# GFNet mixer and gated MLP on one core: one raw-weight subtraction moves behind three unfolding differences in GpSimd's order

## The chip, the cores and the metric

The kernel runs on one core of a Trainium2 chip. The metric is the device time of one execution in microseconds (us). The time before is the median of three executions, 441.07 us, the lowest 440.99 and the highest 441.2.

Engines are named as the profile names them: PE is TensorE's matrix multiplication and PEld its weight load, DVE is VectorE, ACT is ScalarE, POOL is GpSimd and SP is SyncE, which issues the DMAs.

## The reference

The input is 2048 rows of 512 numbers. The first half of the layer normalises the rows, filters them in the frequency domain and adds the input; the second half normalises again and adds a gated MLP.

```python
x = A_x
h = x + irfft2(rfft2(layernorm(x)) * (w_r + 1j * w_i), s=(S, D))     # S, D = 2048, 512
g, u = layernorm(h) @ w_gate, layernorm(h) @ w_up                    # 512 -> 1376
h2 = h + (gelu(g) * u) @ w_down                                      # 1376 -> 512
```

## The kernel before, in words

The 2048 rows are 16 blocks of 128 rows. The Fourier transforms are matrix products with tables of cosines and sines, and symmetries of the tables halve them: sums and differences of the two halves of a row ("folding") are transformed, and the two parts of the result are put together again by sums and differences ("unfolding"). The MLP's hidden width of 1376 is cut into 11 tiles of 128. Products of two-by-two tiles are done with seven products in place of eight, so each tile of gate and up weights needs four sums and differences of the raw weights first (`load_gu`, lines 194 to 229), and then every operand is split into a high and a low part.

The order of the instructions on PE, ACT, DVE and POOL is written out by hand, in strings of short names. `START` orders the forward transform over the rows, `SECOND` the filter and the transform back over the rows, and `FIRST` the transform back over the columns, the second normalisation and the first products of the MLP. A name issues one step; what the steps put on one engine runs in the order of the list. Which instruction waits for which is worked out by the framework from the buffers. SP has its own order, which the framework's scheduler sets.

The change lies in the first line of `FIRST`, where the inverse transform over the columns begins. For a block `b` of rows (0 to 7), in the order in which one needs the other:

- `u`/`w` (two halves) or `U` (whole): the transform of block `b` on PE (L530), 8 instructions in the profile for a whole block, into PSUM bank `k` of `U1.2` (block 1, bank 2).
- `C`: ACT copies the bank into a row buffer (L856).
- `V`: DVE forms one half of the unfolded row from the bank and that copy (L864).
- `X`: POOL forms the other half, a difference, from the copy (L887).
- `M`: PE multiplies the unfolded row by the table `mis` (L869), 2 instructions in the profile, into bank `k` of `M4.1`. It needs both halves, and the bank must have been read by `C` and `V` of the block that had it.
- `O`: ACT copies the odd half of the product (L874); `H`: DVE adds the residual (L879); `G` and `I`: POOL unfolds once more into `gh` (L883).

The names `r0`, `r1`, `r2`, `r3` and `lo1` to `lo3` prepare the third tile of gate and up weights, step by step:

```python
    raw2 = load_gu(2, by=act)
    next(raw2)
    for k in ("r0", "r1", "r2", "r3", "lo1", "lo2", "lo3"):
        do[k] = lambda: next(raw2)
```

The first `next` issues the two DMAs of the tile on SP, 256 KB each (L200, L201), into the single buffer `raw`, which the second tile has used until then: its last read is a split on POOL (L157). Then `r0` is one POOL instruction, the difference of the first column of the raw tile (L207):

```python
        with held("late"):
            pooled["raw"] = i = pool.tensor_tensor(t[:, 4], t[:, 0], t[:, 3], op=ALU.subtract)
```

The next of these names, `r1`, stands far down in the list. `pooled["raw"]` is read again by `late(b)`, which loads a row block for the last stage: its DMA (L975) is made to come behind the newest raw difference.

Of the kernel before, what the change touches and what calls it, by code (L numbers as in the profile page):

```python
# [46 lines left out]
ROOTS = {0: 1, 1: 1, 2: 2, 4: 4, 8: 4, 12: 4}  # L47

FIRST = """
u4.0 w4 u0.1 r0 C4.0 w0 C0.1 U1.2 C1.4 U5.3 C5.5 V4.2 X4 V0.3 X0 M4.1 O4.0 V1.0 M0.2 O0.1 X1 V5.1 X5 H4 G4 H0 I4 U2.3  # L50
C2.5 V2.3 M5.1 U7.2 H5 C7.1 S4 O5.0 G0 A4 g0awh I0 S0 A0 M1.3 O1.1 Q0 U3.4 E0.5 V7.4 X2 C3.5 U6.0 C6.0 N0 R01 I5 R00
H1 G5 S5 X7 M2.1 V6.3 H2 G1 I1 S1 X6 U8.4 C8 T01.2 s0.0 O2.1 l0 T00 A5 A1 c0 V3.1 Q1 M7.0 O7.0 E1.6 U9.7 a0 N1 R10
M6.4 T10 X3 I2 d0 e0.1 k0 H7 H6 f0 g0 b0 h0 U12.3 G2 R11 T11.1 a1 I7 M3.2 C12 U15.3 b1 g0aP0 s1.2 c1 i0 G7 O3.1 O6.0
# [1377 lines left out]
```

## Time and profile before

| | |
|---|---|
| median of three executions | 441.07 us |
| the profiled execution's own time | 440.65 us |
| its span, first to last instruction | 438.4 us |
| PE busy | 432.1 us (99%) |
| POOL busy | 314.3 us (72%) |
| DVE busy | 311.2 us (71%) |
| ACT busy | 244.2 us (56%) |
| granted TensorE clock, mean | 1.000 |

All times of single instructions below come from that one profiled execution and count from its first instruction. A row of a timeline has the start, the duration, the engine, the line of the kernel, the operation, what it writes and reads, and how many instructions of that kind are merged into the row; the bracket at the end is the time for which the engine stood idle before it, and what ended that. An engine named with a q behind it is its queue of waits. A row of the chain of waits has the start, the duration, the engine, the tile and the line.

### The profile page before, as it was taken

The page shows a single profiled execution, that of the slowest core. Times are in us where ns is not written, and L with a number is a line of the kernel's source. Part 1 is how long each engine was busy: PE and PEld are TensorE (multiplying, and loading weights), DVE is VectorE, ACT ScalarE, POOL GpSimd, SP SyncE. Part 2 cuts the span into 40 slices and gives each one's busy share as a digit, 9 for nine tenths or more (in the row PEclk, how much of TensorE's full clock was granted, in tenths as well). Part 3 has the DMA queues.
Part 4 walks back from the last instruction along what each step waited for, and adds up shares of the span by engine and source line. Part 5 has one row for each costly group of instructions (what it writes and reads, how often), then busy time and mean ns, then how long its engine had stood idle before and what let it go on. Part 6 is the DMA issues. An engine that isn't in the chain of part 4 may idle for free.

```text
span 438.4 us, 6627 instructions
## 1 busy us (share of the span) xinstructions
PE 432.1 (99%) x2275; PEld 366.3 (84%) x2275; DVE 311.2 (71%) x576; ACT 244.2 (56%) x505; POOL 314.3 (72%) x346
## 2 busy tenths in 40 slices
PE   8999999999999999999999999999999999999996
PEld 8998999789978777877888888888888888888885
DVE  5968976798764766368734579578677787687786
ACT  5989785699912442124432687376455653565640
POOL 6987896999958788648652944067879779787821
PEclk9999999999999999999999999999999999999999
DMA  8996904320032112112220203501212121200005
GB/s 290 387 414 98 364 22 151 126 73 25 1 120 97 49 49 96 48 49 72 72 73 24 73 25 120 169 9 64 73 48 73 28 70 49 72 25 2 0 2 192
DMA packets 23542, 41.60 MB, mean 95 GB/s; under 512 B 4178, under 2 KB 9810, under 8 KB 23380
## 3 DMA queue, kind: packets, MB, share of 16 engines
q1 hardware_dynamic: 23220, 40.92, 27.8%
q8 instruction: 18, 0.29, 0.3%
q10 hardware_dynamic: 288, 0.26, 0.2%
q14 instruction: 16, 0.13, 0.1%
HBM read 36.97 MB, written 4.20 MB: 94 GB/s over the span
## 4 chain that ended last, share of the span: by engine, by line
PE 92%; ACT 3%; DVE 2%; DMA 1%; issue 1%; POOL 0%; DVEq 0%; POOLq 0%
PE ps L165 16%; PE ps L163 16%; PE ps L164 16%; PE ps L769 14%; PE ps L1108 11%; PE ps L425 4%; PE ps L437 3%; PE ps L530 3%; PE ps L464 3%; PE ps L869 2%; PE ps L977 1%; ACT ts L380 1%; PE ps L1214 1%; DMA gh<-in_x 1%; PE ps L563 1%; PE ps L569 1%
## 5 line engine op out<-in xcount | busy, mean ns | idle before, releaser
L163 PE MATMUL ps<-cb,gu 128*128 128x512 f32 (+1 forms) x336 | 127.4, 379 | 0.0
L165 PE MATMUL ps<-cb,gu 128*128 128x512 f32 (+1 forms) x336 | 124.9, 372 | 0.0
L164 PE MATMUL ps<-cb,gu 128*128 128x512 f32 (+1 forms) x336 | 124.8, 371 | 0.0
L673 ACT ACTIVATE s<-ps 128x512 f32<-128x512 f32 (+1 forms) x72 | 40.2, 560 | 87.5 <-PE ps L165 87.2
L228 POOL TENSOR_TENSOR gu<-raw,gu 128x768 fp32r<-128x768 f32 (+1 forms) x42 | 61.3, 1480 | 29.6 <-DVE gu L223 17.0
L164 PEld LDWEIGHTS ps<-cb,gu 128*128 128x128 f32 x336 | 63.3, 188 | 11.7 <-issue 1.0
L163 PEld LDWEIGHTS ps<-cb,gu 128*128 128x128 f32 x336 | 63.3, 188 | 11.7 <-issue 1.0
L165 PEld LDWEIGHTS ps<-cb,gu 128*128 128x128 f32 x336 | 63.3, 188 | 11.0
L769 PE MATMUL ps<-wd,a 128*128 128x512 f32 x264 | 63.5, 392 | 0.0
L769 PEld LDWEIGHTS ps<-wd,a 128*128 128x128 f32 x264 | 49.2, 188 | 11.5 <-DVE gh L978 0.9
L682 DVE TENSOR_TENSOR ps<-ps,s 128x512 f32<-128x512 f32 (+1 forms) x48 | 31.2, 651 | 27.4 <-PE ps L165 25.3
L1115 DVE TENSOR_TENSOR gh<-ps,gh 128x512 f32<-128x512 f32 x66 | 44.1, 680 | 1.0 <-PE ps L1108 1.0
L679 ACT ACTIVATE s<-s 128x512 f32<-128x512 f32 (+1 forms) x48 | 28.5, 594 | 20.9 <-DVE s L676 20.9
L775 DVE TENSOR_TENSOR gh<-ps,gh 128x512 f32<-128x512 f32 x24 | 16.5, 689 | 27.0 <-PE ps L769 26.9
L676 DVE TENSOR_TENSOR s<-ps,s 128x512 f32<-128x512 f32 (+1 forms) x48 | 30.7, 640 | 5.8 <-PE ps L165 4.7
L511 POOL TENSOR_TENSOR wd<-wdr,wd 128x512 fp32r<-128x512 f32 x12 | 15.5, 1295 | 19.1 <-ACT wd L509 19.1
L676 DVE TENSOR_TENSOR ps<-ps,s 128x512 f32<-128x512 f32 (+1 forms) x24 | 15.7, 653 | 16.8 <-ACT s L673 16.6
L207 POOL TENSOR_TENSOR raw<-raw 128x256 f32<-128x256 f32 x16 | 11.8, 738 | 16.7 <-DMA raw<-in_wgu 15.0
L1021 POOL TENSOR_TENSOR t<-mis,t 128x768 fp32r<-128x768 f32 (+1 forms) x9 | 13.3, 1480 | 13.2 <-ACT t L1019 13.2
L688 ACT ACTIVATE a<-ps 128x512 fp32r<-128x512 f32 (+1 forms) x26 | 13.7, 532 | 15.6 <-DVE ps L682 15.6
L429 ACT ACTIVATE dp<-ps 64x512 f32<-64x512 f32 x32 | 18.9, 591 | 4.1 <-PE ps L425 3.7
L453 POOL TENSOR_TENSOR z<-t,t 128x520 f32<-128x520 f32 x15 | 19.4, 1295 | 2.1 <-DVE t L445 2.1
(183 smaller groups left out, 896.4 us busy)
## 6 DMA issues: line engine op xcount, KB each, us to landing
wt<-in_w SPq DMA_DIRECT2D x16, 520.0 KB, 7.7
raw<-in_wgu SPq DMA_DIRECT2D x32, 256.0 KB, 3.0
out<-gh SPq DMA_DIRECT2D x15, 256.0 KB, 2.0
gh<-in_x SPq DMA_DIRECT2D x7, 512.0 KB, 8.8
row<-in_x SPq DMA_DIRECT2D x12, 256.0 KB, 2.8
wdr<-in_wd SPq DMA_DIRECT2D x12, 256.0 KB, 2.7
mis<-in_wd SPq DMA_DIRECT2D x10, 256.0 KB, 2.6
a<-in_wgu SPq DMA_DIRECT2D x8, 256.0 KB, 3.1
```

What stands on the lines that cost most here:

```text
L163: pe.matmul(o, lh, rh, start=(i == 0 and not onto), stop=False, skip_group_check=True)
L164: pe.matmul(o, lh, rl, start=False, stop=False, skip_group_check=True)
L165: last = pe.matmul(o, ll, rh, start=False, stop=(i == n - 1), skip_group_check=True)
L228: pooled["lo"] = pool.tensor_tensor(r[:, 1, m], t[:, m], r[:, 0, m].bitcast(F32), op=ALU.subtract)
L453: eng.tensor_tensor(z[:, :, first], t1[:, :, first], t2[:, :, first], op=ALU.add)
L673: return lambda: act.activation(to, a, AF.Copy)
L676: return lambda: dve.tensor_tensor(to, a, b, op=ALU.add)
L679: return lambda: act.activation(g, g, AF.Gelu_apprx_tanh)
L682: return lambda: dve.tensor_tensor(u, u, g, op=ALU.mult)
L769: pe.matmul(o, parts_of[tiles.index((0, f))][:, ha, i // 4, r], wds[f][:, hw, c], start=start, stop=stop)
L1108: pe.matmul(ps[:, k], w[:, hw], a[ha], start=start and hw + ha == 0, stop=hw == 1, skip_group_check=True)
L1115: by.tensor_tensor(to, o, to, op=ALU.add)
```

## The change

`r0` moves within the first line of `FIRST`, from a place ahead of `X4`, `X0` and `X1` to a place behind them and ahead of `X5`.

```diff
 FIRST = """
-u4.0 w4 u0.1 r0 C4.0 w0 C0.1 U1.2 C1.4 U5.3 C5.5 V4.2 X4 V0.3 X0 M4.1 O4.0 V1.0 M0.2 O0.1 X1 V5.1 X5 H4 G4 H0 I4 U2.3
+u4.0 w4 u0.1 C4.0 w0 C0.1 U1.2 C1.4 U5.3 C5.5 V4.2 X4 V0.3 X0 M4.1 O4.0 V1.0 M0.2 O0.1 X1 r0 V5.1 X5 H4 G4 H0 I4 U2.3
```

On POOL, at the start of the inverse transform over the columns, this is the order before. `gu_97` is the second weight tile's split, `raw_922` the third tile's raw weights, `row_…` are the row buffers of `X4`, `X0`, `X1` and `X5` in this order, and the `gh` rows are `G4`, `I4`, `G0` and `I0`; the brackets have the engines and DMA queues that a row waits for.

```order
L157 TENSOR_TENSOR gu_97<-raw_584,gu_97 128x256 [waits Activation_49]
L207 TENSOR_TENSOR raw_922<-raw_922 128x256 [waits DMAHW4_49,DMAHW3_49,Pool_49]
L887 TENSOR_TENSOR row_899<-row_897 128x2x128 [waits Activation_49]
L887 TENSOR_TENSOR row_900<-row_898 128x2x128 [waits Activation_49]
L887 TENSOR_TENSOR row_897<-row_901 128x2x128 [waits DVE_49,Activation_49,Pool_49]
L887 TENSOR_TENSOR row_898<-row_902 128x2x128 [waits DVE_49,Activation_49,Pool_49]
L883 TENSOR_TENSOR gh_58<-a_894,t_921 128x256 [waits DMAHW6_49,DVE_49]
```

The same place on POOL in the changed kernel:

```order
L157 TENSOR_TENSOR gu_97<-raw_584,gu_97 128x256 [waits Activation_49]
L887 TENSOR_TENSOR row_899<-row_897 128x2x128 [waits Activation_49]
L887 TENSOR_TENSOR row_900<-row_898 128x2x128 [waits Activation_49]
L887 TENSOR_TENSOR row_897<-row_901 128x2x128 [waits DVE_49,Activation_49,Pool_49]
L207 TENSOR_TENSOR raw_922<-raw_922 128x256 [waits DMAHW4_49,DMAHW3_49]
L887 TENSOR_TENSOR row_898<-row_902 128x2x128 [waits DVE_49,Activation_49,Pool_49]
L883 TENSOR_TENSOR gh_58<-a_894,t_921 128x256 [waits DMAHW6_49,DVE_49]
```

L207 has moved behind three of the L887 rows; it still waits for the two DMAs, and the L887 rows wait for what they waited for.

On SP, the order of the DMAs is the same, and one wait is added. This is the piece of the difference there; `row_1496` is the row block of the first `late`.

```order
 L803 DMA a_894<-in_x 128x512 [waits DMAHW0_49]
 L506 DMA wdr_982<-in_wd 128x512 [waits DMAHW1_49]
-L975 DMA row_1496<-in_x 128x512 [waits DMAHW2_49,PE_49]
+L975 DMA row_1496<-in_x 128x512 [waits DMAHW2_49,PE_49,Pool_49]
 L975 DMA row_1503<-in_x 128x512 [waits DMAHW3_49,DVE_49,Pool_49]
```

The first L975 now waits for POOL as well, that is for L207 in its new place. PE, ACT and DVE have the same rows with the same waits as before.

## The prediction

> **What bounds the kernel now.** I read the page first, then the chain of waits, then the timelines of the engines around the moved instruction. The page says that TensorE is busy throughout and that the chain that ended last is almost wholly its own.
>
> ```profile
> span 438.4 us, 6627 instructions
> PE 432.1 (99%) x2275; PEld 366.3 (84%) x2275; DVE 311.2 (71%) x576; ACT 244.2 (56%) x505; POOL 314.3 (72%) x346
> ...
> PE 92%; ACT 3%; DVE 2%; DMA 1%; issue 1%; POOL 0%; DVEq 0%; POOLq 0%
> ```
>
> So a microsecond counts only where PE waits. The chain of waits between 73 and 80 us has one of its few places where it leaves PE for ACT and POOL, and it is the place of the change:
>
> ```profile
> 74.21 2.96 PE ps L530 x24
> ...
> 77.19 0.61 ACT row L856
> ...
> 77.83 0.42 POOL row L887
> ...
> 78.29 1.98 PE ps L869 x4
> ```
>
> PE's product for block 4 (M4, L869) starts when POOL's first unfolding difference (X4, L887) is done. POOL's timeline shows why that is so late:
>
> ```profile
> 72.34 0.73 POOL L157 TENSOR_TENSOR gu<-raw,gu 128x256 fp32r<-128x256 f32 x1
> 76.82 0.73 POOL L207 TENSOR_TENSOR raw<-raw 128x256 f32<-128x256 f32 x1 [3.76 <-DMA raw<-in_wgu]
> 77.51 2.78 POOL L887 TENSOR_TENSOR row<-row 128x256 f32<-128x256 f32 x4
> 80.70 1.42 POOL L883 TENSOR_TENSOR gh<-a,t 128x256 f32<-128x256 f32 x2 [0.40 <-DVE a L879]
> ```
>
> POOL stands for 3.76 us at r0 (L207), until the raw weights of the third tile have landed at 76.82. Behind it queue the four differences X4, X0, X1 and X5, one every (2.78 - 0.73) / 3 = 0.68 us. The DMA can't come earlier: it waits for the buffer that L157 reads until 73.07, and SP issues it from 73.09.
>
> ```profile
> 73.09 0.33 SPq L200 DMA_DIRECT2D raw<-in_wgu  x1
> 73.46 0.43 SPq L201 DMA_DIRECT2D raw<-in_wgu  x1
> 74.01 1.82 SPq L803 DMA_DIRECT2D a<-in_x  x4
> ...
> 79.45 9.40 SPq L975 DMA_DIRECT2D row<-in_x  x2
> ```
>
> **The change, part by part.** Nothing is added or removed: one POOL subtraction of 0.73 us moves behind X1. What the differences then wait for is ACT's copies (L856: C4, C0, C1, C5 in this order) and, for X5, DVE's half (L864: V4, V0, V1, V5):
>
> ```profile
> 75.41 0.60 ACT L856 ACTIVATE row<-ps 128x512 f32<-128x512 f32 x1 [1.25 <-PE ps L530]
> 76.30 0.60 ACT L856 ACTIVATE row<-ps 128x512 f32<-128x512 f32 x1 [0.30 <-PE ps L530]
> 77.19 0.60 ACT L856 ACTIVATE row<-ps 128x512 f32<-128x512 f32 x1 [0.30 <-PE ps L530]
> 78.08 0.60 ACT L856 ACTIVATE row<-ps 128x512 f32<-128x512 f32 x1 [0.30 <-PE ps L530]
> 79.45 0.38 ACT L874 ACTIVATE t<-ps 128x256 f32<-128x256 f32 x1 [0.77 <-PE ps L869]
> ```
> ```profile
> 76.03 0.42 DVE L864 TENSOR_TENSOR row<-ps,row 128x256 f32<-128x256 f32 x1 [1.43 <-ACT row L856]
> 76.93 0.42 DVE L864 TENSOR_TENSOR row<-ps,row 128x256 f32<-128x256 f32 x1 [0.47 <-ACT row L856]
> 78.27 0.42 DVE L864 TENSOR_TENSOR row<-ps,row 128x256 f32<-128x256 f32 x1 [0.92 <-POOL row L887]
> 78.96 0.42 DVE L864 TENSOR_TENSOR row<-ps,row 128x256 f32<-128x256 f32 x1 [0.26 <-POOL row L887]
> 79.87 1.61 DVE L879 SCALAR_TENSOR_TENSOR a<-a,mv,ps 128x512 f32<-128x512 f32 x2 [0.49 <-ACT t L874]
> ```
>
> The copies end at 76.01, 76.90, 77.79 and 78.68. A consumer starts 0.02 to 0.04 us behind (DVE 76.03 behind 76.01). So X4 runs from 76.05 to 76.78 (it ended at 78.24 before), X0 from 76.94 to 77.67, X1 from 77.83 to 78.56, and V1 and V5, which in the rows waited 0.92 and 0.26 us for POOL, start at 77.83 and 78.72 and end at 78.25 and 79.14. r0 comes next, when its data have been there since 76.82: 78.51 to 79.24, one pitch of 0.68 behind X1. X5 runs from 79.20 to 79.93, where it started at 79.57 and ended at 80.29 before. DVE beside POOL costs nothing extra: V0 at 76.93 ran beside r0 and took 0.42 like V4, which had POOL idle beside it.
>
> X4 is thus no longer what M4 waits for, and what is late next is PE itself. Where PE goes from a transform to a product without a wait, the product starts 0.22 us behind the start of the last transform instruction (80.78 to 81.00), and its two instructions take 0.43 each (81.00 to 81.86). At M4 the last transform instruction started at 77.77:
>
> ```profile
> 77.77 0.28 PE L530 MATMUL ps<-dis,gh 128*128 128x128 f32 x1
> ...
> 78.82 1.45 PE L869 MATMUL ps<-row,mis 128*128 128x512 f32 x3
> ```
> ```profile
> 80.78 0.39 PE L530 MATMUL ps<-dis,gh 128*128 128x128 f32 x2
> ...
> 81.00 1.02 PE L869 MATMUL ps<-row,mis 128*128 128x512 f32 x2
> ...
> 81.86 0.38 PE L530 MATMUL ps<-dis,gh 128*128 128x128 f32 x2
> ```
>
> So M4 starts at 77.99, its second instruction at 78.42 instead of 78.82, M0 at 78.85 and the transform of block 2 at 79.71 where this row has 80.11:
>
> ```profile
> 80.11 1.05 PE L530 MATMUL ps<-dis,gh 128*128 128x128 f32 x8
> ```
>
> **The gain on PE is 0.40 us.** Each cover holds: V0 frees M4's bank at 77.35; M0 needs X0 (77.67) and V1 (78.25), and has until 78.85; the transform of block 2 needs V5 (79.14), and has until 79.71; M5 needs X5, and its weight load stood at 80.89, now 80.49, 0.56 us behind X5's new end. If X1 also had to wait for V1, X5 would end at 80.40, still in time.
>
> The residuals (L879) follow the products: ACT's L874 stood 0.63 behind M4's second instruction, and L879 0.42 behind that, so H4 moves from 79.87 to 79.47, and POOL's L883 from 80.70 to 80.30. POOL is there in time, done with X5 at 79.93. H4 also needs its block of the input, the second of the four L803 transfers, whose landings are in this row:
>
> ```profile
> DMA to landing us min/median/max: 4.2/4.6/4.8
> ```
>
> Landings count from an issue's end (L201's: 73.89 + 2.9 = 76.79, and r0 started at 76.82). The second issue of the four ends near 74.01 + 1.82 / 2 = 74.92; with the median of 4.6 the block is there at 79.5. H4 may so lose 0.05 us, which is hidden: the next L879 on DVE waits for M0's odd half, 0.40 behind M4's.
>
> SP: the first L975 now waits for r0 too, done at 79.24, and for M4, which moves to about 79.05. It is issued at 79.3 instead of 79.45, and the second L975 comes 9 us later anyway. The data of the first are used at 124.91, so even half a microsecond more would cost nothing.
>
> Is the gain given back later? These rows are the busy time by stretches (length; PE, PEld, DVE, ACT, POOL; then granted clock, DMA share and GB/s), the waits of PE from 78 us to the end, and of PEld from 100 us on:
>
> ```profile
> 74.21:78.29 4.08, 3.84 (x32) 3.65 (x33) 1.26 (x4) 2.00 (x4) 1.47 (x3) 1.00 0.92 306
> 78.29:94.40 16.11, 16.11 (x98) 12.09 (x99) 14.41 (x36) 13.00 (x31) 15.49 (x23) 1.00 0.26 85
> ```
> ```profile
> PE ps L869 <- POOL row L887: 0.2, 1, 0.2
> ```
> ```profile
> PEld ps L769 <- DVE gh L978: 0.9, 1, 0.9
> ```
>
> POOL works 15.49 of 16.11 us in the stretch behind the change, so it might have become the bound; but it starts that stretch 0.4 us earlier like PE, and PE waits for nobody. The one later wait of 0.9 us is for DVE's L978, and the chain puts a PE product right ahead of it, so it moves along:
>
> ```profile
> 123.95 0.87 PE ps L977 x2
> ...
> 124.91 0.76 DVE gh L978
> ```
>
> Sum: span 438.4 - 0.4 = 438.0, the profiled execution 440.65 - 0.40 = 440.25. The median of the runs lies 0.42 us above the profiled execution; carried over, 441.07 - 0.40 = **440.67 us**, 0.09% less. A measurement of this kernel can tell about 0.2% (0.88 us) from no change, so this counts as within it.
>
> **What is not known** is when the raw weights land in an ordinary execution. The gain is 0.40 plus what they land later than here, and nothing if they land 0.4 us earlier. The transfers into this buffer around the change took this long, and those of L201 over the whole kernel this long:
>
> ```profile
> DMA to landing us min/median/max: 2.7/2.9/3.7
> ```
> ```profile
> DMA to landing us min/median/max: 3.0/3.1/7.7
> ```
>
> Here it was 2.9. With 2.7 the gain is 0.20, with 3.7 it is 1.20. I take 2.9, this very transfer's.
>
> A rule that speaks against the gain: the Trainium skill, "DMA: Bandwidth & Descriptors", section "Anatomy of one DMA — SWDGE (gpsimd) path", fits a transfer's time as about 2.0 us plus the bytes over 436 GB/s. For 256 KB an estimate by that page is 2.6 us, 0.3 less than the trace's 2.9, and the gain would be 0.10. The fit is for another path of issue and for a transfer alone, so the trace's own duration is used.
>
> **Rivals.**
>
> *Most of the gain isn't there* (gain 0 to 0.25, about 440.95): the transfer lands earlier in ordinary executions, as the shortest of 2.7 would, or PE catches up with POOL's nearly full queue in the stretch from 78.29 to 94.40. For it: 15.49 of 16.11 us busy. Against it: no wait of PE for POOL in that stretch behind M4 and M0. The page's 2.6 us is of this kind.
>
> *The gain is larger* (over 0.88, about 440.0): the transfer is later in ordinary executions; by the 3.7 of the longest into this buffer the kernel before loses 1.20 us and the changed one still nothing, since r0 has until 78.5. For it: the median is 0.42 above the profiled execution. Against it: that may lie anywhere in the kernel.
>
> *Slower:* r0 still waits, now with X5 and the residual's unfolding behind it. M5's weight load stood at 80.89, so X5 must end by 80.84 and r0 start by 79.42; a landing 2.6 us later than here decides. With the longest of L201, 7.7 us, 4.8 more, r0 starts at 81.62, X5 ends 1.41 later at 83.03, and M5 comes 2.2 us later than before: 443.3. For it: r0 stands at the head of POOL's queue all the same, and the DMA engines are 92% busy from 74.21 to 78.29. Against it: the order of the DMAs doesn't change, so nothing new is ahead of this transfer, and with the same lateness the kernel before would have lost more.
>
> *The move has no effect*, since X4 waits for something that r0 waited for too. The order of instructions speaks against it: X4 waits for ACT alone, whose copy was done at 76.01.
>
> **How the numbers follow.** The forecast of 0.25 to 0.88 us gained 0.67; most of the gain absent 0.17; no effect 0.01; larger 0.09; slower by over 0.2% 0.06. That makes faster 0.09, same 0.85, slower 0.06. The range leaves out the slower case and most of the larger one: from a gain of 0.9 to no gain and 0.13 for the spread of the runs before, 440.15 to 441.2.
>
> **What would show it.** In the changed profile L207 starts near 78.5 and waits for no DMA; X4 starts near 76.05 behind ACT's copy; PE has no idle time ahead of L869, and its second instruction starts near 78.42; the first L975 is issued near 79.3; the later stages keep their lengths and the span is 438.0. I am wrong if L869 still waits (then for which half?), if PEld waits for X5 near 80.5, or if a wait of about 0.4 us appears between 80 and 125 us.

## The result, and the profile after

The changed kernel takes 440.28 us (median of 22 executions, 439.98 to 440.93) against 441.03 us of the kernel before (22 executions, 440.66 to 441.46). The ratio is 0.9984 with a 95% interval of 0.9977 to 0.9991: 0.75 us between the medians, 0.4 to 1.0 us by the interval. That is faster, but by less than 0.2%. The prediction had 440.67, in a range from 440.15 to 441.2.

Times below count from S, the start of PE's first transform instruction (L530) of this stage, because S itself moves by a few tenths of a microsecond from one execution to the next whatever the kernel (74.13 to 74.45 us in the profiles here). S is 74.21 in the profile before and 74.45 in the profile after.

POOL in the profile after, from the last split of the second weight tile to the first residual unfoldings:

```profile
72.59 0.72 POOL L157 TENSOR_TENSOR gu<-raw,gu 128x256 fp32r<-128x256 f32 x1
76.32 0.73 POOL L887 TENSOR_TENSOR row<-row 128x256 f32<-128x256 f32 x1 [3.01 <-ACT row L856]
77.22 0.73 POOL L887 TENSOR_TENSOR row<-row 128x256 f32<-128x256 f32 x1 [0.17 <-ACT row L856]
78.17 0.73 POOL L887 TENSOR_TENSOR row<-row 128x256 f32<-128x256 f32 x1 [0.22 <-POOL row L887]
78.85 0.72 POOL L207 TENSOR_TENSOR raw<-raw 128x256 f32<-128x256 f32 x1
79.53 0.73 POOL L887 TENSOR_TENSOR row<-row 128x256 f32<-128x256 f32 x1
80.44 2.79 POOL L883 TENSOR_TENSOR gh<-a,t 128x256 f32<-128x256 f32 x4 [0.17 <-DVE a L879]
```

X4, X0 and X1 now follow ACT's copies, r0 has no wait in front of it, and X5 is done at S + 5.81. PE:

```profile
74.45 3.84 PE L530 MATMUL ps<-dis,gh 128*128 128x128 f32 x32
78.13 1.88 PE L869 MATMUL ps<-row,mis 128*128 128x512 f32 x4
79.85 1.05 PE L530 MATMUL ps<-dis,gh 128*128 128x128 f32 x8
80.74 1.02 PE L869 MATMUL ps<-row,mis 128*128 128x512 f32 x2
```

L869 has lost the idle time in its bracket. The **stretch** from S to the transform behind M0 is 79.85 - 74.45 = 5.40 us, where the profile before had 80.11 - 74.21 = 5.90. The chain of waits goes from the transforms to the products without leaving PE:

```profile
74.45 3.84 PE ps L530 x32
78.29 1.72 PE ps L869 x4
80.01 0.89 PE ps L530 x8
```

Up to DVE's L978, the later wait that the prediction named, nothing is given back: from the transform behind M0 to there it is 124.91 - 80.11 = 44.80 us before and 124.66 - 79.85 = 44.81 after. From the same transform to PE's last group of products (L1214) it is 433.06 - 80.11 = 352.95 us before and 432.94 - 79.85 = 353.09 after, so 0.1 us comes back in the rest of the kernel; why is not shown. First the two rows of the profile before, then those of the profile after:

```profile
124.91 0.75 DVE L978 SCALAR_TENSOR_TENSOR gh<-row,mv,ps 128x512 f32<-128x512 f32 x1 [1.54 <-PE ps L977]
433.06 1.55 PE L1214 MATMUL ps<-a,wd 128*128 128x512 f32 x9
```
```profile
124.66 0.75 DVE L978 SCALAR_TENSOR_TENSOR gh<-row,mv,ps 128x512 f32<-128x512 f32 x1 [1.54 <-PE ps L977]
432.94 1.55 PE L1214 MATMUL ps<-a,wd 128*128 128x512 f32 x9
```

So the mechanism is the one predicted. One number doesn't fit: the stretch is 0.50 us shorter in these two profiles, and the medians are 0.75 us apart.

### The profile page after: what moved, and what is told of

The parts are those of the page before. It is cut to its first block, busy times and chain, and to the rows that moved or that the text cites. A ratio compares the mean times of both kernels' runs of the same rounds, so it can differ in the third digit from the quotient of the medians.

```text
span 438.3 us, 6627 instructions
## 1 busy us (share of the span) xinstructions
PE 432.5 (99%) x2275; PEld 367.0 (84%) x2275; DVE 311.2 (71%) x576; ACT 244.3 (56%) x505; POOL 314.9 (72%) x346
## 4 chain that ended last, share of the span: by engine, by line
PE 92%; POOL 4%; DMA 1%; issue 1%; DVE 1%; ACT 0%; SPq 0%; DVEq 0%
PE ps L163 16%; PE ps L165 16%; PE ps L164 16%; PE ps L769 14%; PE ps L1108 11%; PE ps L425 4%; PE ps L530 3%; PE ps L437 3%; PE ps L464 3%; POOL pn L339 2%; POOL pn L338 2%; PE ps L869 2%; PE ps L977 1%; PE ps L1214 1%; DMA gh<-in_x 1%
## 5 line engine op out<-in xcount | busy, mean ns | idle before, releaser
L207 POOL TENSOR_TENSOR raw<-raw 128x256 f32<-128x256 f32 x16 | 11.8, 737 | 12.9 <-DMA raw<-in_wgu 11.2
```

## Experiments

The theory: M4 waited for X4, X4 for r0, and r0 for the landing of the raw weights; once X4 passes r0, PE sets the pace and nothing is given back. The rivals: r0's own 0.73 us of work was the cost, and not the wait; every difference that passes r0 gives a share, because POOL's queue is what counts; the wait only moves and comes back at X5; and, for the missing 0.25 us, something apart from this edge. Each run was timed beside the kernel before on the same chip (median 441.00 to 441.03 us).

| run | r0 or its stand-in starts, us behind S | stretch, us | median, us | ratio to the kernel before |
|---|---|---|---|---|
| kernel before, four profiles | 2.61, 2.75, 2.86, 3.14 | 5.90, 6.03, 6.15, 6.43 | 441.03 | 1.0001 (0.9992 to 1.0009), run again |
| changed kernel, two profiles | 4.40, 4.39 | 5.40, 5.39 | 440.28, 440.21 | 0.9984 (0.9977 to 0.9991), 0.998 (0.997 to 0.9989) |
| behind_x4 | 3.02 | 5.45 | 440.21 | 0.9979 (0.997 to 0.9989) |
| work_alone | -1.06 | 5.40 | 440.11 | 0.9975 (0.9964 to 0.9986) |
| wait_alone | 3.06 | 5.81 | 440.52 | 0.9984 (0.9975 to 0.9993) |
| late_old | 3.79 | 7.07 | 441.31 | 1.0005 (0.9996 to 1.0014) |
| late_new | 4.39 | 5.39 | 439.83 | 0.9974 (0.9964 to 0.9984) |
| behind_x5 | 5.29 | 5.39 | 440.10 | 0.9981 (0.9972 to 0.999) |
| behind_i0 | 8.71 | 5.39 | 440.72 | 0.9995 (0.9985 to 1.0004) |
| far_back | after this stage | 5.40 | 440.11 | 0.9979 (0.997 to 0.9988) |

The medians hold 2.2 us that lie outside the span of the instructions, but 1.8 to 1.9 us in work_alone, wait_alone and far_back and 2.1 us in the two late runs. In the profiles of the first three the span also goes on for 3.4 us behind the last output's issue (L1220) instead of 3.1, so their medians come out about 0.1 us low. The cause of this is open; where a median and the stretch differ by as little, the stretch is the safer measure.

### The changed kernel once more

No edit.

> The changed kernel once more, beside the runs below on one chip. Theory (M4 waited for X4, X4 for r0): PE comes from the first transform instruction (L530) to the transform behind M0 in 5.40 us again, where the kernel before takes 5.90, and the time is 0.5 to 0.75 us under the kernel before. Rival (the 0.75 us of the medians holds something besides this edge): the stretch is 5.40 us again, and the time still lies 0.25 us or more further down than the stretch explains.

Measured: stretch 5.39 us, 440.21 us, 0.82 us under the kernel before. The stretch is the theory's. The time lies 0.32 us further down than this stretch and the first profile's 5.90 explain, which is what the rival asked for; the profiles of the kernel before, below, show where that comes from.

### Which difference has to pass r0

```diff
-... V4.2 X4 V0.3 X0 M4.1 O4.0 V1.0 M0.2 O0.1 X1 r0 V5.1 X5
+... V4.2 X4 r0 V0.3 X0 M4.1 O4.0 V1.0 M0.2 O0.1 X1 V5.1 X5
```

> r0 stands behind X4 alone, ahead of X0, X1 and X5. Theory (only the edge from X4 to M4 counts): X0 ends near the time at which X4 ended before, 0.6 us ahead of M0's need, so the stretch is 5.40 us and the time that of the changed kernel, within 0.15 us. Rival (every difference that passes r0 gives its share, since POOL's queue is what counts): a third of the gain, 0.2 us, and two thirds are lost.

Measured: 440.21 us, the changed kernel's time, and a stretch of 5.45. POOL's rows in this run:

```profile
76.02 0.72 POOL L887 TENSOR_TENSOR row<-row 128x256 f32<-128x256 f32 x1 [3.01 <-ACT row L856]
77.16 0.73 POOL L207 TENSOR_TENSOR raw<-raw 128x256 f32<-128x256 f32 x1 [0.42 <-DMA raw<-in_wgu]
77.84 2.11 POOL L887 TENSOR_TENSOR row<-row 128x256 f32<-128x256 f32 x3
```

r0 waits for its DMA again, 0.42 us, and X0, X1 and X5 stand behind it; X0 ends at S + 4.4, only 0.1 us ahead of M0's start where 0.6 was expected, and the stretch is 0.05 us longer. The gain comes with X4. Shares per difference are out. But the landing still stands ahead of X0 in this order, and here it let r0 start at S + 3.02: a later one, such as the S + 3.14 of one profile below, would reach M0 through X0. That is an estimate from these rows; no run shows it.

### The work without the wait, and the wait without the work

Both put a stand-in `rx` into r0's old place, with r0 in its new one. The first subtracts data that are there already, and r0 overwrites its result; the second subtracts two columns of the raw tile:

```diff
-u4.0 w4 u0.1 C4.0 w0 C0.1 ...
+u4.0 w4 u0.1 rx C4.0 w0 C0.1 ...
...
+do["rx"] = lambda: pool.tensor_tensor(rt[:, 4], <mis[:, 0:2]>, <mis[:, 2:4]>, op=ALU.subtract)    # work_alone
+do["rx"] = lambda: pool.tensor_tensor(rt[:, 4, :2], rt[:, 0, :2], rt[:, 3, :2], op=ALU.subtract)   # wait_alone
```

> The changed kernel with one more subtraction of the size of r0 in r0's old place, of data that are there already (two rows of the table mis), so the work stands there without the wait for the DMA; its result is overwritten by r0. Theory: it runs at once, near 73 us, three microseconds ahead of X4, and the time is that of the changed kernel, within 0.15 us. Rival (the 0.73 us of work on POOL ahead of X4 are the cost): 0.5 us or more above the changed kernel.

Measured: 440.11 us, stretch 5.40. The work runs where POOL stood idle, and X4 starts at 76.07 - 74.20 = S + 1.87, as in the changed kernel:

```profile
73.14 0.72 POOL L945 TENSOR_TENSOR raw<-mis 128x256 f32<-128x256 f32 x1
76.07 0.72 POOL L887 TENSOR_TENSOR row<-row 128x256 f32<-128x256 f32 x1 [2.21 <-ACT row L856]
```

The work alone costs nothing.

> The changed kernel with a subtraction of two columns of the raw tile in r0's old place, so the wait for the DMA stands there with 0.2 us of work in place of 0.73. Theory: X4 starts near 77.0 on the clock of the profile before and ends near 77.75, just ahead of the 77.85 at which PE is free for M4, so the stretch is 5.40 to 5.50 us and the time 0 to 0.2 us above the changed kernel (more in executions in which the data land later). Rival (the wait is the whole cost, the work none): X4 is late as in the kernel before and the time is the kernel before's, 0.5 to 0.75 us above the changed one.

Measured: 440.52 us, 0.51 under the kernel before and 0.24 to 0.31 above the two medians of the changed kernel; stretch 5.81. The transfer was late in this profile, and the stand-in started at 77.20 - 74.14 = S + 3.06:

```profile
77.20 0.20 POOL L945 TENSOR_TENSOR raw<-raw 128x2 f32<-128x2 f32 x1 [4.21 <-DMA raw<-in_wgu]
77.35 2.10 POOL L887 TENSOR_TENSOR row<-row 128x256 f32<-128x256 f32 x3
79.40 0.74 POOL L207 TENSOR_TENSOR raw<-raw 128x256 f32<-128x256 f32 x1
80.08 0.74 POOL L887 TENSOR_TENSOR row<-row 128x256 f32<-128x256 f32 x1
```
```profile
78.13 1.98 PE L869 MATMUL ps<-row,mis 128*128 128x512 f32 x4 [0.15 <-POOL row L887]
```

X4 starts at S + 3.21, where the profile before had S + 3.30 with an earlier landing. Neither number is hit: the theory had counted on the landing of the first profile, and with the rival the time would be the kernel before's. What fits both kernels is the sum. M4 starts at the landing, plus the time that r0 or its stand-in holds POOL (0.69 and 0.15 us), plus 0.78 us from X4's start to M4's: 2.61 + 0.69 + 0.78 = 4.08 in the profile before, 3.06 + 0.15 + 0.78 = 3.99 here, as measured. PE would be ready at S + 3.68. By the same sum a wait with no work behind it would put M4 at 3.39 with the landing of the first profile and at 3.92 with the latest of the four below, on time or 0.24 us late: the loss was the wait and r0's work together (an estimate from these rows). Behind M4, the stand-in's lateness reaches PE a second time: X5, now behind r0, ends at 80.82, and M5 starts at 80.88. That costs another 0.14 us, so in this run the wait does come back at X5, as one rival said.

### The landing later, with r0 in its old and in its new place

One more DMA of 128 KB ahead of L201, into a column that isn't in use yet:

```diff
-nc.sync.dma_start(t[:, :2], wgu[f, :, :2])
+nc.sync.dma_start(t[:, :2], wgu[f, :, :2]), more and nc.sync.dma_start(t[:, 6], wgu[f, :, 1])
...
-raw2 = load_gu(2, by=act)
+raw2 = load_gu(2, by=act, more=True)
```

> r0 in its old place, and one more DMA of 128 KB into a column of the raw tile that is not yet in use, issued ahead of L201, so the raw weights land some 0.45 us later (one issue). Theory: X4 and M4 move by as much; the stretch grows from 5.90 to about 6.35 us and the time is 0.3 to 0.6 us above the kernel before. Rival (M4 was late for another reason): no change against the kernel before.

Measured: the landing came 1.18 us later than in the first profile, not 0.45, and the stretch grew by 1.17 us, to 7.07:

```profile
77.99 0.72 POOL L207 TENSOR_TENSOR raw<-raw 128x256 f32<-128x256 f32 x1 [4.93 <-DMA raw<-in_wgu]
```
```profile
79.45 1.98 PE L869 MATMUL ps<-row,mis 128*128 128x512 f32 x4 [1.40 <-POOL row L887]
```

In the trace PE follows the landing one for one. The median, 441.31 us, is only 0.28 above the kernel before, just outside what was expected; part of the reason is in the next run.

> The same additional DMA with r0 in its new place. Theory: r0 starts behind X1 near 78.5 with the data there since about 77.3, so nothing waits; the four x blocks land 0.45 us later too, which reaches H4 by at most 0.1 us; the time is that of the changed kernel, 0.5 to 0.75 us under the kernel before. Rival (the wait is only moved and comes back at X5): the time is that of the kernel before or above it.

Measured: stretch 5.39 with the same additional transfer, so r0 in its new place doesn't pass the lateness on. The x blocks did: H4 (L879) came late, POOL waited 0.79 us for it, and the next product on PE 0.21 us. G4 (L883) starts at S + 6.59 instead of S + 5.99, so H4 lost 0.6 us where the expectation had put 0.1 at most:

```profile
80.86 2.78 POOL L883 TENSOR_TENSOR gh<-a,t 128x256 f32<-128x256 f32 x4 [0.79 <-DVE a L879]
```
```profile
80.93 1.10 PE L869 MATMUL ps<-row,mis 128*128 128x512 f32 x2 [0.21 <-DVE a L879]
```

The transform behind it starts at S + 7.60, 0.45 us later than in the changed kernel, and yet the median is 439.83 us, 0.4 us under that kernel's. Part of this lies far away: DVE stands idle for 0.48 us ahead of L1034 in the changed kernel's second profile, and doesn't with the additional DMA, and the chain of waits passes one group of PE's L1108 0.24 us faster. The two go together in every profile: both late runs have no such idle time and 0.68 us for this group, the other twelve 0.48 to 0.50 and 0.89 to 0.92; that one causes the other isn't shown. First DVE's row and PE's piece of the chain in the changed kernel (the chain is that of its first profile), then those of late_new:

```profile
423.58 0.69 DVE L1034 TENSOR_TENSOR a<-ps,a 96x512 fp32r<-96x512 f32 x1 [0.48 <-issue]
```
```profile
430.13 0.92 PE ps L1108 x3
```
```profile
423.63 0.69 DVE L1034 TENSOR_TENSOR a<-ps,a 96x512 fp32r<-96x512 f32 x1
```
```profile
430.34 0.68 PE ps L1108 x3
```

Another 0.1 us lies outside the span. And the profiled execution of late_new, 440.28 us, is one of three of its eight at 440.24 to 440.31; the other five took 439.60 to 439.92, and no profile shows one of these. Why the stall goes, and what the five had less, stays open. The two late runs can be compared with one another all the same: 441.31 - 439.83 = 1.48 us between the medians, and between the profiles 7.07 - 5.39 = 1.68 us less the 0.45 that H4 cost, 1.23. r0's new place takes most of the lateness away.

### Further back

```diff
-... X1 r0 V5.1 X5 H4 G4 H0 I4 ... S4 O5.0 G0 A4 g0awh I0 S0
+... X1 V5.1 X5 H4 G4 H0 I4 ... S4 O5.0 G0 A4 g0awh I0 r0 S0       # behind_i0
+... X1 V5.1 X5 r0 H4 G4 H0 I4 ... S4 O5.0 G0 A4 g0awh I0 S0       # behind_x5
```

far_back has `r0` just ahead of `r1`, 29 POOL instructions further down the list; the scheduler then also issues the two L975 later.

> r0 stands further back, behind X5 and the four residual unfoldings. Theory: PE waits for none of them, so the time is that of the changed kernel, within 0.15 us. Rival (POOL's nearly full queue behind X1 costs something, so r0 ahead of X5 and G4 is still in the way): another 0.2 us or more gained.

Measured: 440.72 us, 0.44 to 0.51 us above the changed kernel. Both were wrong: the theory, which saw no cost, and the rival, which saw a gain. The stretch is 5.39 and PE runs like the changed kernel up to S + 16; then it waits. These are POOL's rows, a wait of DVE that the changed kernel doesn't have, PE here, and PE in the second profile of the changed kernel:

```profile
82.96 0.74 POOL L207 TENSOR_TENSOR raw<-raw 128x256 f32<-128x256 f32 x1
83.65 0.75 POOL L887 TENSOR_TENSOR row<-row 128x256 f32<-128x256 f32 x1
```
```profile
DVE bn L520 <- POOL gh L883: 0.4, 1, 0.4
```
```profile
90.66 0.55 PE L563 MATMUL ps<-ident,a 128*128 128x128 f32 x3 [0.33 <-ACT a L912]
```
```profile
90.18 0.65 PE L563 MATMUL ps<-ident,a 128*128 128x128 f32 x4
```

r0 pushes every POOL instruction behind it 0.5 to 0.7 us back. The unfolding (L883) is late for the statistics (L520), these for the normalised rows (L912), and these for PE's transposes (L563), which stood at 90.18 - 74.27 = S + 15.91 in the second profile of the changed kernel and stand at 90.66 - 74.25 = S + 16.41 here. So POOL does have little room in this stage.

> r0 stands behind X5 and ahead of the first residual unfolding G4, one place further back than in the changed kernel and four places ahead of the run behind_i0, which lost 0.5 us against the changed kernel. Theory (POOL's queue from G4 on has about 0.2 us of room before PE waits at L563 for the normalised rows; ahead of G4 POOL stands idle for 0.65 us in behind_i0, waiting for H4): r0's 0.69 us fit into that idle time but for 0.04 us, so the time is that of the changed kernel, within 0.15 us. Rival (any place behind X5 costs what behind_i0 cost): 0.4 to 0.5 us above the changed kernel.

Measured: 440.10 us, stretch 5.39. One place behind X5 costs nothing, since POOL would wait for H4 there:

```profile
78.73 0.73 POOL L887 TENSOR_TENSOR row<-row 128x256 f32<-128x256 f32 x1 [0.17 <-POOL row L887]
79.42 0.73 POOL L207 TENSOR_TENSOR raw<-raw 128x256 f32<-128x256 f32 x1
80.11 2.79 POOL L883 TENSOR_TENSOR gh<-a,t 128x256 f32<-128x256 f32 x4
```

The first L883 starts at S + 5.98, as in the changed kernel (S + 5.99), where it waited 0.17 us for H4.

> r0 stands just ahead of r1, some twenty POOL instructions further back, behind the stretch in which POOL has no room. Theory: G4 starts behind H4 as in the changed kernel and PE waits nowhere more, so the time is that of the changed kernel within 0.15 us; the DMAs of L975 come later, which costs nothing as their data are needed 45 us later. Rival (every us of work taken out of that stretch of POOL is a gain): 0.3 us or more below the changed kernel.

Measured: 440.11 us. POOL then idles in this place, and nothing more is won:

```profile
80.30 2.78 POOL L883 TENSOR_TENSOR gh<-a,t 128x256 f32<-128x256 f32 x4 [0.65 <-DVE a L879]
```

### The kernel before, three more profiles

No edit. The second was timed too; the third and fourth are one execution each.

> The kernel before once more, for another profile of it. Both theories: no difference in time. Theory (the landing of the raw weights sets the loss, and it varies): POOL's wait at r0 again ends at a landing, and the stretch from PE's first L530 to the transform behind M0 is 5.90 us give or take what the landing moves, 0.1 to 0.4 us. If the stretch is longer than 5.90 here, the ordinary loss is larger than the first profile showed.

> The kernel before, for a third profile. Theory (the loss is 0.5 us plus what r0 starts later than 2.61 us behind PE's first transform instruction): r0 starts 2.6 to 3.1 us behind it, and the stretch is 5.90 us plus the difference, to 0.05 us. Rival (the loss doesn't follow the landing): the stretch stays near 5.9 to 6.0 whatever the start of r0.

> The kernel before, for a fourth profile, with the same expectation as the third: the stretch from PE's first L530 to the transform behind M0 is 5.90 us plus what r0 starts later than 2.61 us behind it. If the mean over the four profiles of the kernel before stays near 2.7, the 0.75 us between the medians isn't explained by the landing and stays open; if it is near 2.85, it is.

Measured: r0 started 2.61, 2.75, 2.86 and 3.14 us behind S in the four profiles, and the stretch was 5.90, 6.03, 6.15 and 6.43 us, each 3.28 or 3.29 us more. The latest of them:

```profile
77.46 0.72 POOL L207 TENSOR_TENSOR raw<-raw 128x256 f32<-128x256 f32 x1 [4.29 <-DMA raw<-in_wgu]
78.14 2.79 POOL L887 TENSOR_TENSOR row<-row 128x256 f32<-128x256 f32 x4
```
```profile
78.92 1.98 PE L869 MATMUL ps<-row,mis 128*128 128x512 f32 x4 [0.77 <-POOL row L887]
```

SP issued the two DMAs at the same places in all four, 1.11 to 1.12 and 0.74 to 0.75 us ahead of S. The first profile, on which the prediction was built, had the earliest landing of the four. The mean stretch is 6.13 us, 0.73 above the changed kernel's 5.40. Less the 0.1 us that comes back behind it (352.95 to 352.98 us to L1214 in these four, 353.09 and 353.06 in the changed kernel's two profiles), that is 0.6 of the 0.75 us between the medians, within their interval of 0.4 to 1.0.

The rest may be no more than which executions were profiled. The four took 440.65, 440.74, 440.99 and 441.28 us, in the order of their stretches; less the stretch that is 434.75, 434.71, 434.84 and 434.85, so the landing is nearly all that sets them apart. By that an execution of the median time, 441.03 us, has a stretch of about 6.24 us (an estimate), 0.84 above the changed kernel's, and with 0.1 given back 0.7 remains. Four profiles are few; but with the slope of one in all four, and in late_old as well, no second cause is needed, and a small one isn't excluded.

## Why the prediction was right, and where it was off

- **The bound and the edge** were right, and the size was not: 0.40 us was forecast and 0.75 measured, inside the range but near its lower end in time. PE set the end but for one wait, M4 for X4; behind_x4 shows that the gain comes with X4 passing r0, late_old that PE follows the landing one for one, and work_alone that r0's work is free where POOL is idle.
- **X4, X0, X1, r0 and X5** start at S + 1.87, 2.77, 3.72, 4.40 and 5.08; the prediction's times, less its S of 74.21, are 1.84, 2.73, 3.62, 4.30 and 4.99. X1 is 0.1 us later than worked out, and the two behind it follow; X5 had 0.56 us of cover, and PE didn't wait for it.
- **PE's step from transform to product** was mis-sized: 0.22 us, where the runs show 0.11. The row that starts at 80.78 holds two transform instructions, and the start of the first was taken for that of the last. In the profile after, the last of the 32 starts at S + 3.57 and M4 at S + 3.68. PE came out 0.50 us ahead in the profiles instead of 0.40.
- **The landing** was the other term that was too small. The prediction called the ordinary landing unknown, priced both sides, and took this one profile's own. It is the earliest of four, and the mean is 0.23 us later. 0.40 + 0.10 + 0.23 = 0.73 us. There was a sign of it: the prediction saw that the profiled execution lay 0.42 us below the median, and set it aside since that may lie anywhere in the kernel. By the estimate above, 6.24 - 5.90 = 0.34 us of that lay in this landing.
- **Given back later** was put at nothing. That holds up to L978; over the rest of the kernel 0.1 us comes back, at no wait that the profile names.
- **The row of landings was a poor measure** of that. It says 2.9 us for this transfer in the first profile and in the fourth, whose r0 started 0.53 us later behind S; the wait in POOL's own row is what moved.
- **The Trainium skill's fit** ("DMA: Bandwidth & Descriptors", section "Anatomy of one DMA — SWDGE (gpsimd) path", about 2.0 us plus the bytes over 436 GB/s, an estimate of 2.6 us here) would have made the gain 0.10. The trace disagrees: r0 started 3.36, 3.49, 3.60 and 3.89 us behind the start of L201's issue in the four profiles, and 2.93, 3.06, 3.17 and 3.46 us behind its end, from which the prediction counted.
- **L975's added wait** cost nothing: it was issued at S + 5.15, where 5.1 was predicted.
- **POOL's queue** was left out as a bound because PE starts the stage earlier together with POOL. That holds for this change. The prediction named POOL's nearly full queue as a rival and found no wait of PE in it; behind_i0 shows how near that limit is, since the same instruction a few places further back costs 0.5 us there.
- **The slower rival** did not come about: r0 in its new place waited for no DMA, not even with the additional transfer in late_new. A landing late enough for it was in no profile.

No version is clearly better than the changed kernel: behind_x4, behind_x5, work_alone and far_back lie within 0.2 us of it. The median of late_new is 0.4 us lower, for reasons that are partly open, and with a transfer that nobody needs, and no profile shows its faster executions.

## What to carry to other kernels

In an engine that works through its queue in order, look for an instruction that waits for a DMA and has urgent work behind it; the first urgent instruction is the one that has to pass it, those behind it only as far as a late transfer would reach them, and the best place for the waiting one is where the engine would wait for something else anyway. The price of such a wait varies from run to run with the transfer, so a single profile gives one draw of it: take a second profile before sizing the gain. Moving it further back isn't free by itself, since a few places on, the same 0.7 us may stand in a stretch without room.

## What the runs showed of the hardware that was not expected

- The same two transfers, issued at the same place of the program, let r0 start 2.61 to 3.14 us behind S in four executions of one kernel, a spread of 0.53 us.
- One additional transfer of 128 KB ahead of it, which took one more issue on SP (0.47 us), moved that start by 0.65 to 1.18 us, to 3.79.
- DVE's idle time of 0.48 us ahead of L1034, 350 us further on, in which it waits for nothing that the profile shows, is in twelve of the fourteen profiles (0.48 to 0.50 us) and went away with that transfer in both late runs. What it is stays open.
